# Recurrent attention and a gated MLP on one core: scores and the state's product in one stretch, placed between the two groups of y

## The chip, the cores and the metric

The kernel runs on one core of a Trainium2 chip. The core has five engines that work side by side: TensorE (PE, matrix products into PSUM), VectorE (DVE), ScalarE (ACT), GpSimd (POOL) and SyncE (SP, which issues the DMAs). Each runs its own list of instructions in order, and waits on semaphores where it needs another engine's result. The metric is the device time of one execution in microseconds, the median of several runs.

## The reference

For 4 sequences, 8 heads, 768 positions and head size 48, a state of 48x48 per head is carried along the positions; the result is the input of a gated MLP with mixing over positions (gMLP, d_model 384, d_ff 1024):

```
for t in range(S):
    cur = einsum('bhd,bhe->bhde', u * k_t, v_t)
    y[t] = einsum('bhd,bhde->bhe', r_t, state + cur)
    state = w_t[..., None] * state + einsum('bhd,bhe->bhde', k_t, v_t)
x = y, heads side by side                      # (4, 768, 384)
h = gelu(x @ w_in);  u, v = halves of h
v_n = (v - mean) / sqrt(var + 1e-6) * g_ln
v_s = einsum('ts,bsd->btd', w_sg, v_n) + b_sg
out = x + (u * v_s) @ w_out
```

## The kernel before

**Steps.** The recurrence is cut into chunks of 128 positions: 6 per sequence, 24 steps in all, counted from 0 (step n is chunk n % 6 of sequence n // 6). A chunk has two halves of 64 positions. The 8 heads lie as 4 pairs, one head of a pair in partitions 0 to 63, the other in 64 to 127. Per step:

- loads of w, of k and r (KR), of v, and from step 6 on of k and r once more in another layout (RK, for the "own weights");
- `decays`, `decayed_k`: two scans over the decays on DVE (lines 430 and 435), then k and r multiplied by their decays (lines 459 and 437, DVE or POOL);
- `own_weights`: the term u*k*r of each position with itself. For the first ON_PE["own"] steps one product on DVE or POOL and 4 matmuls (line 473), after that three elementwise operations on RK. The result fills the diagonal of the tile `a`;
- `scores`: 16 matmuls of 64x64 (k against r, line 506) into the PSUM buffer a_ps; then DVE copies what lies under the mask into `a` (line 508);
- `state`: 4 transposes of k (line 520) into k_ps, a copy to SBUF (kt), 16 matmuls of 64x48 (kt against v, line 529) into a_ps, and three operations of DVE or POOL: S1 = product of the first half + S2 (line 540), T2 = S1 times a decay (line 546), S1' = product of the second half + T2 (line 552). `decayed` makes the next step's S2 from S1' (line 565 or 563). On the chip each matmul of this data type gives two records in the trace, so 16 matmuls are 32 records;
- `outputs`: y in one PSUM buffer, in two groups. The first group is 8 matmuls of `a` and v (line 581); the second is 8 or 16 matmuls of the states S2 and T2 with r (line 602) and 8 more of `a` and v (line 581). Between the groups a copy of one column of y, the "look" (line 593, on ACT or DVE; a copy helper, so the trace shows it as line 283) is awaited by PE, so that the second group starts only when the first can be read. Three copies then take y to SBUF.

a_ps is a single buffer of two banks, taken twice per step: once by the scores, once by the state's product. kt is a single buffer too.

**gMLP.** Each product in full precision is made of three passes (lines 681 to 683) over matmuls of 128x128 weights and 384 or 512 columns, in three PSUM buffers (m_ps). `v_piece`: the v half of one chunk, GELU and normalisation; `u_piece`, `gate_piece` (18 passes over all six v of a sequence), `out_piece` with its final sum on DVE (line 779, into one of two buffers o) and the DMA out (line 781). The weights come in as 64-bit numbers and are split into a high and a low part; for the first ON_PE["w"] of ten weights the low part is gathered by three passes on PE (lines 816 to 818) and a copy, for others by two elementwise operations on POOL or DVE (lines 823 and 825).

**What sets the order.** All this is written as generators that yield operations (`Op`) with a cost per engine, events they wait for, and buffers they take. `Plan.run` keeps a clock per engine and always picks the operation that can start first; among those that can start within 0.02 us of each other the lower rank wins. A step's rank is n - LEAD of its sequence; gMLP pieces have ranks from the constants FIRST and PIECE, weights from WEIGHT. The order so found is fixed at build time; on the chip each engine follows it. `small` marks stretches of 64x64 matmuls: in the plan the first such operation after a full matmul costs 0.1 us more. `_, done, e_...` are events; an operation sees another's result `LAT` after its end (0.3 us after PE, 0.2 after others).

Of the kernel before, what the change touches and what calls it, by code (L numbers as in the profile page):

```python
# [14 lines left out]
ALU = mybir.AluOpType  # L15
# [4 lines left out]
B, H, S, D = 4, 8, 768, 48  # L20
C = 128
T = 64
NC = S // C
NP = H // 2
# [11 lines left out]
LEAD = (2.97, 1.57, 3.33, 2.58)  # L36
FIRST = {"v": -1.8, "u": 4.09, "gate": 1.92, "out": 6.86}
PIECE = {"v": 1.71, "u": 3.76, "gate": 4.87, "out": 1.55}
WEIGHT = {"v": -10.85, "u": -4.28, "sg0": 2.68, "sg1": -0.01, "out": -0.36, "g": 4.14}

BIAS = {"DVE": 0.07, "POOL": -0.09}
# [33 lines left out]
class Op:  # L75
# [3 lines left out]
    def __init__(self, on, after=(), take=(), free=(), done=None, kb=None, two=False, apart=False, small=False, slack=0.0):  # L79
        self.on, self.after, self.take, self.free, self.done, self.kb = on, after, take, free, done, kb  # L80
        self.two = two
        self.slack = slack
        self.small = small
        self.apart = apart
# [6 lines left out]
class Event:  # L91
    t = None

# [35 lines left out]
class Plan:  # L129
# [13 lines left out]
    def cost(self, op, e, t):  # L143

        c = op.on[e]
        if e == "PE":
            c = (2 * c if t < COLD else c) + (0.1 if op.small and not (self.pe_last and self.pe_last.small) else 0.0)
        return c

    def add(self, rank, gen):  # L150
        self.count += 1
        p = [rank, gen, 0.0, None, self.count]
        self.procs.append(p)
        self._next(p, None)
# [7 lines left out]
    def run(self):  # L162
        while True:
            best = {}
            for p in self.procs:
                op = p[3]
                if any(e.t is None for e in op.after) or any(len(s.free) < op.take.count(s) for s in op.take):
                    continue
                ready = max([p[2]] + [e.t for e in op.after] + [s.since(op.take.count(s)) for s in op.take])
                _, t, e = min((s + self.cost(op, e, s) + BIAS.get(e, 0.0), s, e) for e in op.on  # L170
                              for s in (max(ready, self.engines[e], self.port if op.port(e) else 0.0),))
                best.setdefault(e, []).append((t, p[0], p[4], p))
# [24 lines left out]
            if op.done is not None:  # L197
                op.done.t = op.seen
            if not op.apart:
                p[2] = op.seen  # L200
# [75 lines left out]
def rwkv_gmlp(ctx: ExitStack, tc: tile.TileContext, wpad, kr, vtok, ktok, vt, u, ucol, w_in, g_ln, w_sgT, b_sg, w_out, out):  # L276
# [5 lines left out]
    def copy(e, o, i):  # L282
        nc.scalar.copy(o, i) if e == "ACT" else engine[e].tensor_copy(o, i)  # L283
# [103 lines left out]
    ch = [Part("W", "KR", "V", "RK", "own", "k", "r", "suf", "pre", "pc", "A", "M", "S1", "S2", "T2", "ym", "y") for _ in steps]  # L387
# [74 lines left out]
    def own_weights(n):  # L462

        x = ch[n]
        if n < ON_PE["own"]:
# [4 lines left out]
            op = yield Op({"PE": 0.8}, small=True, after=[e_uc], take=[m_m], free=[rk])  # L470
# [27 lines left out]
    def scores(n):  # L498

        x = ch[n]  # L500
        op = yield Op({"PE": 0.62}, small=True, after=[x.e_k, x.e_r], take=[m_a])
        a_ps, = op.got
        x.kr.done(op.seen)
        for p, j, c_ in [(p, j, c_) for p in range(NP) for j in range(2) for c_ in range(2)]:
            k_, r_ = (x.KR[64 * j:64 * j + 64, i, p * C + c_ * T:p * C + c_ * T + T] for i in range(2))
            nc.tensor.matmul(a_ps.tile[64 * c_:64 * c_ + 64, j, p * T:(p + 1) * T], k_, r_, start=True, stop=True)  # L506
        yield Op({"DVE": 0.64}, after=[x.e_A], free=[a_ps], done=x.e_M)
        nc.vector.copy_predicated(x.a.tile.rearrange("s j p t -> s j (p t)"), mask, a_ps.tile[:, :, 0:NP * T])

    def state(n):  # L510
# [4 lines left out]
        m = T if last else C  # L515
        op = yield Op({"PE": 0.37}, after=[x.e_k], take=[m_s])
        kt_ps, = op.got
        x.kr.done(op.seen)
        for p in range(NP):
            nc.tensor.transpose(kt_ps.tile[0:m, p], x.KR[:, 0, p * C:p * C + m], ident)  # L520
        op = yield Op({"ACT": 0.5, "DVE": 0.61}, take=[s_kt], free=[kt_ps])
        kt, = op.got
        copy(op.e, kt.tile[0:m], kt_ps.tile[0:m])
        op = yield Op({"PE": 0.4 if last else 0.62}, small=True, after=[x.e_V], take=[m_a], free=[kt])
        ds, = op.got
        x.v.done(op.seen)
        for p, c_, j in [(p, c_, j) for p in range(NP) for c_ in range(1 if last else 2) for j in range(2)]:
            h = 2 * p + j
            nc.tensor.matmul(ds.tile[64 * j:64 * j + 64, c_, p * 64:p * 64 + D],  # L529
                             kt.tile[64 * c_:64 * c_ + 64, p, 64 * j:64 * j + 64],  # L530
                             x.V[64 * c_:64 * c_ + 64, h * D:(h + 1) * D], start=True, stop=True)
        ds_ps = [ds.tile[:, c_, 0:NP * 64].rearrange("d (p e) -> d p e", e=64)[:, :, 0:D] for c_ in range(2)]
        ds.n = 1 if last else 2
        mid = ds_ps[0]
        if g > 0:
            op = yield Op({"DVE": 0.27}, after=[x.e_S2], take=[s_S1], free=[ds])
            S1, = op.got
            mid = S1.tile
            x.S2.done(op.seen)
            nc.vector.tensor_tensor(mid, ds_ps[0], x.S2.tile[:, :, 0:D], ALU.add)  # L540
        op = yield Op({"DVE": 0.3, "POOL": 0.6} if g else {"DVE": 0.3}, after=[x.e_pc], take=[s_S2], done=x.e_T2,
                      free=[S1 if g else ds], two=g > 0)
# [3 lines left out]
        engine[op.e].tensor_tensor(x.T2.tile[:, :, 0:D], mid,  # L546
                                   x.pc.tile[:, :, 1].unsqueeze(2).broadcast_to([128, NP, D]), ALU.mult)
        if not last:
            op = yield Op({"DVE": 0.27}, take=[s_S1], free=[ds], done=x.e_S1)
            x.S1, = op.got  # L550
            x.T2.done(op.seen)
            nc.vector.tensor_tensor(x.S1.tile, ds_ps[1], x.T2.tile[:, :, 0:D], ALU.add)
# [16 lines left out]

    def outputs(n):  # L570
# [15 lines left out]
        op = yield Op({"PE": 0.36}, small=True, after=[x.e_M, x.e_V, *turn], take=[m_y])  # L586
# [179 lines left out]
    def out_piece(b, half, i):  # L766
# [10 lines left out]
        op = yield Op({"DVE": 0.48}, take=[s_o], free=[m, h_.x])  # L777
# [117 lines left out]
    for n, (b, g) in enumerate(steps):  # L895
# [6 lines left out]
        for f in (decays, range_check, chunk_pc, decayed_k, own_weights, state, decayed, scores, outputs):  # L902
            if f is decayed and g == 0:
                continue
            plan.add(r, f(n))
# [210 lines left out]
```

## Time and profile before

| | |
|---|---|
| time, median of 3 runs | 391.02 us (389.45 to 391.55) |
| time of the profiled execution | 392.47 us |
| its span, first to last instruction | 390.6 us |
| granted TensorE clock, mean | 0.994 |
| PE busy | 363.0 us (93%), 4513 matmul records |
| weight loads (PEld) busy | 317.2 us (81%) |
| DVE, ACT, POOL busy | 292.1 (75%), 193.2 (49%), 93.7 us (24%) |
| HBM read and written | 43.19 and 4.72 MB |

The span counts from the first to the last instruction of the program; the time of an execution holds a little more around it. Busy is the share of time in which at least one instruction of the engine is drawn. Matmuls are pipelined, so two of them overlap in the drawing; the distance from start to start tells more than the duration.

### The profile page before, as it was taken

To read this page: it belongs to the slowest core of one execution; us is meant where nothing else is said; L and a number is where in the kernel's file an instruction comes from. 1 tells how busy PE (TensorE), PEld (TensorE's weight loads), DVE (VectorE), ACT (ScalarE), POOL (GpSimd) and SP (SyncE) were. 2 spreads that over 40 slices of the span, in tenths; PEclk is the share of its full clock that TensorE was granted. 3 is DMA by queue.
4 is the path that set the end of the run, shared out by engine and by line. 5 is a ranking of instruction groups with operands and counts; after the bars stand their busy time and mean duration, and the time that the engine had idled before them with its cause. 6 is when DMAs were issued, how large, how long until landed. Compare 5 with 4: busy or idle time off the path is not lost.

```text
span 390.6 us, 10968 instructions
## 1 busy us (share of the span) xinstructions
PE 363.0 (93%) x4513; PEld 317.2 (81%) x4513; DVE 292.1 (75%) x588; ACT 193.2 (49%) x502; POOL 93.7 (24%) x121
## 2 busy tenths in 40 slices
PE   1989899799989999999999999999999999989992
PEld 1756678588879978978799988878999889979991
DVE  7999998699999979998999797487732545452251
ACT  3659676785432565666344166563444744521010
POOL 6124441233142254225540332032000002100000
PEclk9999999999999999999999999999999999999997
DMA  8776558624356254663323713122325510000101
GB/s 264 275 235 195 165 152 287 205 88 143 86 171 213 64 160 147 225 220 100 120 90 128 229 48 121 45 76 90 112 94 184 160 56 25 3 1 20 42 1 67
DMA packets 23961, 49.87 MB, mean 128 GB/s; under 512 B 3808, under 2 KB 12768, under 8 KB 23904
## 3 DMA queue, kind: packets, MB, share of 16 engines
q1 hardware_dynamic: 23904, 49.10, 38.4%
q8 instruction: 37, 0.61, 0.6%
q14 instruction: 20, 0.16, 0.1%
HBM read 43.19 MB, written 4.72 MB: 123 GB/s over the span
## 4 chain that ended last, share of the span: by engine, by line
PE 70%; DVE 17%; DMA 6%; ACT 3%; issue 2%; ACTq 0%; DVEq 0%
PE m_ps L681 20%; PE m_ps L683 17%; PE m_ps L682 17%; PE a_ps L506 3%; PE y_ps L581 3%; PE a_ps L529 2%; PE y_ps L602 2%; DVE m_ps L757 2%; PE k_ps L520 2%; DMA u<-in_w_sgT 2%; DVE W L435 2%; DVE a L495 2%; DVE W L430 1%; DMA x<-y 1%; DMA KR<-in_kr 1%
## 5 line engine op out<-in xcount | busy, mean ns | idle before, releaser
L681 PE MATMUL m_ps<-wsgh,vn 128*128 128x384 f32 x192 | 67.9, 353 | 2.6 <-DVE g L763 2.6
L683 PE MATMUL m_ps<-wsgh,vn 128*128 128x384 f32 x192 | 64.7, 337 | 0.1
L682 PE MATMUL m_ps<-wsgl,vn 128*128 128x384 f32 x192 | 64.6, 336 | 0.0
L681 PEld LDWEIGHTS m_ps<-wsgh,vn 128*128 128x128 f32 x192 | 36.0, 188 | 5.6 <-DVE g L763 3.6
L761 ACT CAST g<-m_ps 128x384 fp32r<-128x384 f32 x32 | 15.2, 480 | 44.9 <-DVE m_ps L759 44.6
L683 PEld LDWEIGHTS m_ps<-wsgh,vn 128*128 128x128 f32 x192 | 36.1, 188 | 0.4 <-DVE vn L723 0.4
L682 PEld LDWEIGHTS m_ps<-wsgl,vn 128*128 128x128 f32 x192 | 36.1, 188 | 0.3
L712 POOL TENSOR_TENSOR st<-st,mhalf 128x1 f32<-128x1 f32 x24 | 20.4, 853 | 62.3 <-DVE st L710 50.6
L757 DVE SCALAR_TENSOR_TENSOR m_ps<-m_ps,g_ln,b_bc 128x384 f32<-128x384 f32 x32 | 19.3, 619 | 20.0 <-PE m_ps L683 20.0
L681 PE MATMUL m_ps<-g,wouth 128*128 128x384 f32 x96 | 34.0, 354 | 0.0
L681 PE MATMUL m_ps<-xT,winh 128*128 128x384 f32 x96 | 33.5, 348 | 0.1
L446 ACT ACTIVATE junk<-W 128x1040 f32<-128x1040 f32 x24 | 25.8, 1073 | 14.9 <-DVE W L435 12.2
L682 PE MATMUL m_ps<-g,wouth 128*128 128x384 f32 x96 | 32.5, 338 | 0.5 <-DVE g L763 0.5
L683 PE MATMUL m_ps<-xT,winl 128*128 128x384 f32 x96 | 32.4, 337 | 0.0
L683 PE MATMUL m_ps<-g,woutl 128*128 128x384 f32 x96 | 32.3, 337 | 0.0
L682 PE MATMUL m_ps<-xT,winh 128*128 128x384 f32 x96 | 32.3, 337 | 0.0
L430 DVE TENSOR_TENSOR_SCAN W<-W,D 128x520 f32<-128x520 f32 x24 | 30.8, 1283 | 1.7 <-DMA W<-in_wpad 1.7
L737 ACT ACTIVATE u<-m_ps 128x384 f32<-128x384 f32 x32 | 15.6, 490 | 31.8 <-PE m_ps L683 31.7
L435 DVE TENSOR_TENSOR_SCAN W<-W,D 128x520 f32<-128x520 f32 x24 | 31.1, 1297 | 0.1
L681 PE MATMUL m_ps<-winh,xT 128*128 128x512 f32 x72 | 31.1, 432 | 0.2 <-DVE g L763 0.2
L683 PE MATMUL m_ps<-winh,xT 128*128 128x512 f32 x72 | 28.6, 397 | 0.8 <-ACT xT L283 0.8
L682 PE MATMUL m_ps<-winl,xT 128*128 128x512 f32 x72 | 28.4, 394 | 0.0
(151 smaller groups left out, 837.6 us busy)
## 6 DMA issues: line engine op xcount, KB each, us to landing
KR<-in_kr SPq DMA_DIRECT2D x24, 512.0 KB, 4.2
RK<-in_ktok SPq DMA_DIRECT2D x18, 384.0 KB, 3.7
W<-in_wpad SPq DMA_DIRECT2D x24, 260.5 KB, 3.6
vtok<-in_vtok SPq DMA_DIRECT2D x24, 192.0 KB, 4.2
out<-o SPq DMA_DIRECT2D x24, 192.0 KB, 1.9
vn<-in_w_in SPq DMA_DIRECT2D x6, 512.0 KB, 6.1
KR<-in_w_in SPq DMA_DIRECT2D x6, 512.0 KB, 3.8
u<-in_w_sgT SPq DMA_DIRECT2D x12, 192.0 KB, 3.9
```

The source lines that it names most:

```text
L430: nc.vector.tensor_tensor_scan(Suf[:, WL - 1:0:-1], W[:, WL - 1:0:-1], D1[:, WL - 1:0:-1], 0.0, ALU.mult, ALU.add)
L435: nc.vector.tensor_tensor_scan(W[:, 0:WL - 1], W[:, 0:WL - 1], D2[:, 0:WL - 1], 0.0, ALU.mult, ALU.add)
L446: nc.scalar.activation(junk.rearrange("p (a x) -> p a x", a=2), both, AF.Square, accum_out=chk[:, n:n + 1])
L506: nc.tensor.matmul(a_ps.tile[64 * c_:64 * c_ + 64, j, p * T:(p + 1) * T], k_, r_, start=True, stop=True)
L581: nc.tensor.matmul(place(j, q, r, c_), x.V[64 * c_:64 * c_ + 64, h * D:h * D + 64], x.a.tile[64 * c_:64 * c_ + 64, j, p], start=(start and ...
L681: nc.tensor.matmul(ps, lh, rh, start=(i == 0), stop=False)
L682: nc.tensor.matmul(ps, lh, rl, start=False, stop=False)
L683: nc.tensor.matmul(ps, ll, rh, start=False, stop=(i == n - 1))
L712: nc.gpsimd.tensor_tensor(rstd, var, c.mhalf, ALU.pow)
L737: nc.scalar.activation(h_.u[f].tile, ps, AF.Gelu_apprx_tanh)
L757: nc.vector.scalar_tensor_tensor(ps, ps, c.g[:, d:d + 1], c.b_bc[:, ts], ALU.mult, ALU.add)
L761: nc.scalar.copy(gh, ps)
```

## The change

The scores and the state's product of a step become one operation, `products`: 32 matmuls back to back into one a_ps buffer (scores in the first half of each bank, the state's product in the second). The transposes and the copy kt become an operation of their own (`turned_k`), the masked copy another (`masked`). For steps 0 to 9 (JOINED = 9) `first_products` runs the products by themselves. For the later ones they are part of `outputs` of the step before: from step 9 on the order on PE is first group of y of step n, products of step n+1, second group of y of step n, each marked `next_to` (rank lowered by 100). For this the first group also waits for all that the second group and the products need. The look is a process of its own, with its rank lowered by 50.

In the planner, an operation that follows one on its own engine may start at that one's end, without the latency; entering a small stretch costs 0.2; constants are new. One more step has its own weights on PE, two weights fewer have their low part there. The last half's outputs use buffers of u in place of o.

```diff
-ON_PE = {"own": 6, "x": 5, "w": 10}
+JOINED = 9
+ON_PE = {"own": 7, "x": 5, "w": 8}
...
-            c = (2 * c if t < COLD else c) + (0.1 if op.small and not (self.pe_last and self.pe_last.small) else 0.0)
+            c = (2 * c if t < COLD else c) + (0.2 if op.small and not (self.pe_last and self.pe_last.small) else 0.0)
...
-                ready = max([p[2]] + [e.t for e in op.after] + [s.since(op.take.count(s)) for s in op.take])
+                ready = max([0.0] + [s.since(op.take.count(s)) for s in op.take])
                 _, t, e = min((s + self.cost(op, e, s) + BIAS.get(e, 0.0), s, e) for e in op.on
-                              for s in (max(ready, self.engines[e], self.port if op.port(e) else 0.0),))
-                best.setdefault(e, []).append((t, p[0], p[4], p))
+                              for s in (max([ready, self.engines[e], self.port if op.port(e) else 0.0, p[2].on(e)]
+                                            + [x.on(e) for x in op.after]),))
+                best.setdefault(e, []).append((t, p[0] - (100.0 if op.next_to else 0.0), p[4], p))
...
+    def products(n, op):
+        x = ch[n]
+        last = steps[n][1] == NC - 1
+        x.ps, = op.got
+        ps, kt = x.ps.tile, x.kt.tile
+        for p, j, c_ in [(p, j, c_) for p in range(NP) for j in range(2) for c_ in range(2)]:
+            k_, r_ = (x.KR[64 * j:64 * j + 64, i, p * C + c_ * T:p * C + c_ * T + T] for i in range(2))
+            nc.tensor.matmul(ps[64 * c_:64 * c_ + 64, j, p * T:(p + 1) * T], k_, r_, start=True, stop=True)
         for p, c_, j in [(p, c_, j) for p in range(NP) for c_ in range(1 if last else 2) for j in range(2)]:
             h = 2 * p + j
+            nc.tensor.matmul(ps[64 * j:64 * j + 64, c_, NP * T + p * T:NP * T + p * T + D],
+                             kt[64 * c_:64 * c_ + 64, p, 64 * j:64 * j + 64],
                              x.V[64 * c_:64 * c_ + 64, h * D:(h + 1) * D], start=True, stop=True)
+        for buf in (x.kr, x.v, x.kt):
+            buf.done(op.seen)
+        x.ps.n = 2 if last else 3
+
+    ready = lambda n: [ch[n].e_k, ch[n].e_r, ch[n].e_V, ch[n].e_kt]
...
+        with_it = ready(n + 1) if n + 1 < N else []
...
-        op = yield Op({"PE": 0.36}, small=True, after=[x.e_M, x.e_V, *turn], take=[m_y])
+        joined = n >= JOINED
+        final = [x.e_T2, x.e_r, *([x.e_S2] if g else [])]
+        op = yield Op({"PE": 0.27}, small=True, after=[x.e_M, x.e_V, *turn, *([*final, *with_it] if joined else [])],
+                      take=[m_y])
...
-        op = yield Op({"ACT": 0.2, "DVE": 0.1}, take=[s_look])
-        look, = op.got
-        copy(op.e, look.tile, y.tile[0][:, 1, C - 1:C])
-        look.done(op.seen)
-        op = yield Op({"PE": 0.87 if g else 0.63}, small=True, after=[x.e_T2, x.e_r, *([x.e_S2] if g else [])],
-                      done=x.e_ym)
+        e_look = Event()
+        plan.add(rank(n) - 50.0, look(y, e_look, op.seen))
+        if joined and with_it:
+            op = yield Op(time(n + 1), small=True, take=[m_a], done=ch[n + 1].e_sd, next_to=True)
+            products(n + 1, op)
+        op = yield Op({"PE": 0.79 if g else 0.55}, small=True, after=[e_look, *final], done=x.e_ym, next_to=joined)
...
-        op = yield Op({"DVE": 0.48}, take=[s_o], free=[m, h_.x])
+        op = yield Op({"DVE": 0.48}, take=[s_u if h_.n == N - 3 else s_o], free=[m, h_.x])
```

## Rows read from the trace of the kernel before

**Rows 1.** Busy time by engine in three windows: stretch, length, busy (x instructions), clock, DMA.

```profile
0.00:62.00 62.00, 48.84 (x834) 36.40 (x835) 58.17 (x108) 39.91 (x111) 23.20 (x39) 1.00 0.67 220
62.00:200.00 138.00, 133.11 (x1912) 115.14 (x1911) 126.69 (x248) 77.15 (x203) 45.22 (x50) 1.00 0.47 152
200.00:320.00 120.00, 119.83 (x1439) 107.57 (x1438) 80.48 (x171) 58.28 (x148) 21.28 (x26) 1.00 0.34 112
```

**Rows 2.** Waits of PE: who waited for whom, us in total, times, longest.

```profile
PE m_ps L681 <- DVE g L763: 2.8, 4, 1.6
...
PE y_ps L581 <- DVE a L508: 1.2, 2, 0.9
```

**Rows 3.** Timeline of PE about a first group of y: start, us drawn, instruction.

```profile
182.85 0.34 PE L682 MATMUL m_ps<-wsgl,vn 128*128 128x384 f32 x1
183.02 0.34 PE L683 MATMUL m_ps<-wsgh,vn 128*128 128x384 f32 x1
183.29 0.46 PE L581 MATMUL y_ps<-a,vtok 64*64 64x64 f32 x16
...
183.96 0.34 PE L682 MATMUL m_ps<-wsgl,vn 128*128 128x384 f32 x1
```

**Rows 4.** Timeline of PE about a second group of y that stands alone.

```profile
212.86 0.34 PE L683 MATMUL m_ps<-wsgh,vn 128*128 128x384 f32 x1
213.12 0.69 PE L602 MATMUL y_ps<-KR,S 64*64 64x64 f32 x32
213.64 0.41 PE L581 MATMUL y_ps<-a,vtok 64*64 64x64 f32 x16
...
214.26 0.34 PE L682 MATMUL m_ps<-wsgl,vn 128*128 128x384 f32 x1
```

**Rows 5.** Timeline of PE where a state's product stands between the groups of y.

```profile
167.59 0.46 PE L581 MATMUL y_ps<-a,vtok 64*64 64x64 f32 x16
167.87 0.63 PE L529 MATMUL a_ps<-vtok,kt 64*64 64x48 f32 x32
168.42 0.69 PE L602 MATMUL y_ps<-KR,S 64*64 64x64 f32 x32
168.91 0.44 PE L581 MATMUL y_ps<-a,vtok 64*64 64x64 f32 x16
```

**Rows 6.** Timeline of PE: the second group of y of steps 5 and 23.

```profile
63.74 0.69 PE L602 MATMUL y_ps<-KR,S 64*64 64x64 f32 x32
...
316.46 0.69 PE L602 MATMUL y_ps<-KR,S 64*64 64x64 f32 x32
```

**Rows 7.** Timeline of PE: own weights of a step, and one weight of w_out.

```profile
46.46 0.95 PE L473 MATMUL m_ps<-u_col,RK 128*128 128x8 f32 x8
...
70.92 0.91 PE L816 MATMUL m_ps<-g,ident 128*128 128x384 f32 x2 [1.71 <-ACT u L737]
...
72.02 0.34 PE L681 MATMUL m_ps<-xT,winh 128*128 128x384 f32 x1
```

**Rows 8.** Two lines' instructions: count, ns min/median/max, first and last start.

```profile
L676 DVE TENSOR_TENSOR xT<-x,xT x19: 508/551/1067, 77.9 to 329.7; 128x384 fp32r<-128x384 f32 x19
...
L481 POOL TENSOR_TENSOR RK<-RK,u_bc x11: 997/1027/1471, 74.4 to 204.5; 128x384 f32<-128x384 f32 x11
```

**Rows 9.** Timeline of PE, DVE and ACT: a first group of y, two looks.

```profile
171.31 0.46 PE L581 MATMUL y_ps<-a,vtok 64*64 64x64 f32 x16
...
172.60 0.14 DVE L283 COPY look<-y_ps 128x1 f32<-128x1 f32 x1
...
183.82 0.16 ACT L283 COPY look<-y_ps 128x1 f32<-128x1 f32 x1 [1.05 <-PE y_ps L581]
```

**Rows 10.** Timeline of all engines at the end.

```profile
382.70 0.34 PE L683 MATMUL m_ps<-g,woutl 128*128 128x384 f32 x1
383.76 0.56 DVE L779 TENSOR_TENSOR o<-m_ps,x 128x384 f32<-128x384 f32 x1 [2.24 <-DMA out<-o]
```

**Rows 11.** Timeline of DVE: the last normalised v.

```profile
342.86 0.69 DVE L723 TENSOR_TENSOR vn<-v,vn 128x512 fp32r<-128x512 f32 x1 [0.69 <-ACT vn L283]
```

More of the change, by code (lines that the diff above doesn't have):

```diff
@@ L75, with __init__ @@
 class Op:
-    def __init__(self, on, after=(), take=(), free=(), done=None, kb=None, two=False, apart=False, small=False, slack=0.0):
+    def __init__(self, on, after=(), take=(), free=(), done=None, kb=None, two=False, apart=False, small=False, slack=0.0,
+                 next_to=False):
         self.on, self.after, self.take, self.free, self.done, self.kb = on, after, take, free, done, kb
         self.two = two
+        self.next_to = next_to
         self.slack = slack
@@ L196, in run @@
                 b.done(op.seen)
[L197 to L200, printed above, removed]
+            for x in [p[2]] * (not op.apart) + [op.done] * (op.done is not None):
+                x.t = op.seen
+                if op.kb is None:
+                    x.e, x.end = e, op.end
             self.log.append((t, op.end, e, p[0], p[1].__name__))
@@ L496, in own_weights, with turned_k @@
                                        diag.unsqueeze(1).unsqueeze(1).broadcast_to([128, 2, NP, T]), ALU.mult)
-    def scores(n):
+    def turned_k(n):
         x = ch[n]
-        op = yield Op({"PE": 0.62}, small=True, after=[x.e_k, x.e_r], take=[m_a])
-        a_ps, = op.got
+        m = T if steps[n][1] == NC - 1 else C
+        op = yield Op({"PE": 0.37}, after=[x.e_k, *([ch[n - 1].e_kt] if n else [])], take=[m_s])
+        kt_ps, = op.got
         x.kr.done(op.seen)
+        for p in range(NP):
+            nc.tensor.transpose(kt_ps.tile[0:m, p], x.KR[:, 0, p * C:p * C + m], ident)
+        op = yield Op({"ACT": 0.5, "DVE": 0.61}, take=[s_kt], free=[kt_ps], done=x.e_kt)
+        x.kt, = op.got
+        copy(op.e, x.kt.tile[0:m], kt_ps.tile[0:m])
@@ new lines, in products, with first_products, masked @@
+        for buf in (x.kr, x.v, x.kt):
+            buf.done(op.seen)
+        x.ps.n = 2 if last else 3
+    ready = lambda n: [ch[n].e_k, ch[n].e_r, ch[n].e_V, ch[n].e_kt]
+    time = lambda n: {"PE": 0.78 if steps[n][1] == NC - 1 else 1.02}
+    def first_products(n):
+        op = yield Op(time(n), small=True, after=ready(n), take=[m_a], done=ch[n].e_sd)
+        products(n, op)
+    def masked(n):
+        x = ch[n]
+        op = yield Op({"DVE": 0.64}, after=[x.e_A, x.e_sd], done=x.e_M)
+        x.ps.done(op.seen)
+        nc.vector.copy_predicated(x.a.tile.rearrange("s j p t -> s j (p t)"), mask, x.ps.tile[:, :, 0:NP * T])
@@ L568, in decayed, with look @@
         x.pc.done(op.seen)
+    def look(y, done, t):
+        e = Event()
+        e.t = t
+        op = yield Op({"ACT": 0.2, "DVE": 0.1}, take=[s_look], after=[e], done=done)
+        look, = op.got
+        copy(op.e, look.tile, y.tile[0][:, 1, C - 1:C])
+        look.done(op.seen)
     def outputs(n):
@@ L901, in rwkv_gmlp @@
             plan.add(FIRST_LOADS.get((n, f.__name__), r), f(n))
-        for f in (decays, range_check, chunk_pc, decayed_k, own_weights, state, decayed, scores, outputs):
-            if f is decayed and g == 0:
+        for f in (decays, range_check, chunk_pc, decayed_k, turned_k, own_weights, first_products, masked, state, decayed,
+                  outputs):
+            if f is decayed and g == 0 or f is first_products and n > JOINED:
                 continue
```

66 lines of the change are left out of this document (27 added, 39 removed).

## The prediction

> **What bounds the kernel now.** I read the windows of three stretches first. TensorE (PE) is busy 133.11 of 138 us between 62 and 200 us and 119.83 of 120 us between 200 and 320 us, at the full granted clock, while VectorE (DVE) falls from 126.69 of 138 to 80.48 of 120 [rows 1]. Before 62 us PE has gaps (48.84 of 62), since inputs and decays are still arriving. The list of waits agrees: of PE's later waits the largest is 2.8 us in all, for the gate's product g, and for the step's own operands y waited 1.2 us [rows 2]. So from about 62 us on PE always has a gMLP product ready, and time taken out of PE's queue there comes off the end. A busy share can't say how much is useful, though: a 384-column product is drawn 0.34 us long but the next one starts 0.17 us later [rows 3]. I therefore go by starts.
>
> The timeline of PE shows what small products cost beside their own work. Small ones (64 rows by 64 columns) stand in stretches between full ones (128 by 128). Within a stretch they start 0.016 us apart (32 in 213.12 to 213.64, [rows 4]). The first group of y, alone, takes from 183.02 to 183.96, the starts of the full product before it and of the second one after it: 0.94 us. Two full ones take 2 x 0.17, the 16 small ones 16 x 0.016 = 0.26, and 0.34 is left over [rows 3]. The second group, 48 small ones alone: 1.40 - 0.34 - 0.77 = 0.29 [rows 4]. Both ends are one price: entering and leaving a stretch costs about 0.31 us, however long it is.
>
> One place already looks as the changed kernel will: at 167.59 the state's product stands directly between the two groups of y, and 16 + 32 + 32 products go from 167.59 to 168.91, 1.32 us or 0.04 over 80 x 0.016 [rows 5]. Two seams, 0.02 each. Joining two stretches therefore saves 0.31 - 0.02 = 0.29 us.
>
> **The change part by part.** *Stretches.* Steps are counted from 0. From the second group of y of step 5 at 63.74 to the last at 316.46 I count 61 stretches of small products between full ones [rows 6]. Up to four per step: scores, state's product, first and second group of y; some touch by chance. In the changed kernel the same part holds: the second y of step 5, two groups each for steps 6 to 8, one stretch of products each for steps 6 to 9 (11 in all); one stretch each for steps 9 to 22 with the products of the next step inside (14); two groups of step 23. That is 27. Chance merges among the 11 may take 2 away, and some of the 14 will be split because a condition isn't met in the plan (4 more). I take 29, with 25 and 45 as ends. 61 - 29 = 32 stretches x 0.29 = 9.3 us less. The number of small products, of transposes and of DVE's instructions per step is the same, and so are their times.
>
> *Before 62 us* there were 16 stretches, where PE waits anyway. Scores now also wait for the turned k and for v, and the state's product for r. I cost this at nothing, hidden by those 13.2 us of gaps, with 2 us either way; a gain or a loss there ends in the same idle time.
>
> *Fewer weights on PE* (10 to 8). Two of w_out lose three passes: 70.92 to 72.02 is 1.10 us each [rows 7], 2.2 us less on PE. In their place come two elementwise operations each (lines 823 and 825), which no row of before shows. The nearest are a 128x384 subtraction on DVE, 0.55 us, and a 128x384 product on GpSimd, 1.03 us [rows 8], so 2.2 us of DVE or 4.1 of GpSimd, less one copy each. Neither is on the path: nothing asks for w_out before the first output product, and PE has other work. Bounds 0 and +2.2, I take 0.
>
> Beside GpSimd's work that DVE row goes up to 1.07 us from a median of 0.55 [rows 8]. The Trainium skill (SBUF — State Buffer, Who interferes with whom) says why: a DVE instruction with two inputs in SBUF is kept out while a GpSimd instruction that reads SBUF runs, for its whole length. The trace agrees in kind; by that rule alone DVE would lose up to the 4.1 us, and 4.1 us more on the end if DVE set it.
>
> *Own weights of step 6 on PE* (6 to 7): eight more products, 0.95 us [rows 7], against a DMA of 384 KB and two elementwise operations less. +0.95.
>
> *The look* (the one-column copy that PE awaits between the groups of y) had other full products as cover; now it has the 64 products, 64 x 0.016 = 1.0 us. An early one starts 0.53 us after its group's start and is done at 183.98, 0.69 after it [rows 3, 9], and the first group itself lasts 0.26, so 0.43 is needed of 1.0. The late one ran on DVE at 172.60, behind a copy, its group having begun at 171.31; it is done at 172.74, 1.43 after [rows 9]: that would leave PE idle 1.43 - 0.26 - 1.0, about 0.2 us plus the way back. Of the 15 looks from step 9 on this was the only late one. I allow 14 x 0.02 = 0.3.
>
> *The joint gate.* The first group of y of step n now waits for what the second needed (the state before and in the middle of the chunk) and for k, r, v and the turned k of step n+1, and the buffer must be free of its three readers. PE works in order, so every full product behind a gate that is late waits, and after it the copies out of the three m_ps buffers. The rows give 0.9 us as the longest such wait for y [rows 2]. Steps are 14 us apart (18 between 63.74 and 316.46, [rows 6]) and only three or four DVE operations lie between products and gate, so the gate is normally met long ahead. I allow 0.7 us in all; bounds 0 and 14 x 0.45 (half of the longest) = 6.3.
>
> *The order* is made anew with other constants, and an operation after one on its own engine no longer counts a latency. What can be won so is PE's idle time from 62 to 320 us, 4.9 + 0.2 = 5.1 us [rows 1]; what can be lost I put into the rivals. I take 0.
>
> *The end.* The last sum of the output waits for a buffer that a DMA holds: DVE starts at 383.76, the last product ended at 382.70 + 0.34 = 383.04 [rows 10]. With the last half's outputs in the eight u buffers it starts at once: 0.7 us less. What follows (DMA out, closing waits) stays.
>
> Sum: -9.3 - 2.2 + 0.95 + 0.3 + 0.7 - 0.7 = -10.25. The profiled execution took 392.47 us (span 390.6 and 1.9 around it), so 382.2; it was 1.45 above the median of the runs, 391.02. From the median: 380.8 us.
>
> **The rivals.**
> *D, stretches not whole.* The planner takes whatever can start first; when the buffer or the look is a moment late, full products slip in and a joint stretch falls into two or three. The many chance splittings of before speak for it, and that the new operations get precedence once ready speaks against. With half of the gain: 16 x 0.29 = 4.6, so 385.4.
> *B, waits at the gate.* All the stretches come whole, but 14 gates or looks cost 0.45 us rather than 0.07: 5.3 back, 386.1. For it: a static order with ten conditions at one point; against: a single long wait for y in the trace.
> *E, no change.* D and B together: 4.7 + 5.3 back, 390.8.
> *C, slower: DVE takes over the path between 62 and 200 us.* It has 11.3 us free there [rows 1]; a PE that is some 6 us ahead brings gMLP's sums and casts forward into the same stretch, the two w_out weights add theirs, and the step's mask and state sums then come in one burst after the products, on which the next gate hangs. Then the attention falls behind, and the last y is late. After it comes a chain that can't be moved: the last normalised v is ready at 342.86 + 0.69 = 343.55 [rows 11], and 39.5 us of gate and output products follow up to 383.04. From the last y (ends about 317.3) to 343.55 are 26 us; I put half of them, 13 us, down as slack (an estimate). So the kernel becomes slower than before only if the last y comes after about 333 us. At 336 the span is 336 + 13 + 39.5 + 6.9 = 395.4, and the time 395.4 + 1.9 - 1.45 = 396. Against it: DVE has 39.5 us free from 200 to 320 to catch up. The rule of the Trainium skill cited above belongs here; by its 4.1 us alone that point would not be reached.
>
> **How the numbers follow.** Forecast 0.60, D 0.13, B 0.13, E 0.06, C 0.08. I call 0.5% (2 us) no change, what a measurement here can tell. Faster by more: 0.60 + 0.13 + 0.13 = 0.86; within: 0.06; slower: 0.08. The forecast's own range is 377 to 384 (28 or 36 stretches saved, 2 us at the start, a part of the 5.1 us of idle time). The range of 8 in 10 takes in D and B and reaches towards E: 375.5 to 389.
>
> **What would show it.** In the timeline of PE: 27 to 33 stretches of small products after the second y of step 5, and from step 9 on the row order y, scores, state, y with no full product between; starts within it 0.016 us apart. PE's busy time down by some 9 to 11 us, its products' number down by two weights' passes and up by eight. No idle row before L581 or the second group beyond 0.5 us. The last y near 306 us; the last output sum right behind its product. Wrong would be: over 40 stretches (D), idle rows summing over 4 us at y (B), DVE without gaps and the last y after 325 us (C), or a stretch price that doesn't go away when stretches are joined.

## The result and the profile after

The changed kernel takes 385.86 us (median of 4 runs, 385.12 to 387.65), the kernel before 391.05 (4 runs): ratio 0.9881, 95% interval 0.9836 to 0.9926. It is faster by 5.2 us, half of the 10.25 us forecast. The profiled execution took 385.56 us with a span of 383.9.

The page of the changed kernel, busy time by engine, and its windows (columns as in [rows 1]):

```profile
PE 353.7 (92%) x4513; PEld 317.6 (83%) x4513; DVE 307.0 (80%) x593; ACT 191.5 (50%) x507; POOL 106.4 (28%) x144
```

```profile
0.00:62.00 62.00, 45.72 (x672) 32.86 (x675) 56.57 (x99) 27.41 (x67) 19.21 (x36) 0.92 0.59 198
62.00:200.00 138.00, 132.61 (x2069) 119.56 (x2062) 134.37 (x257) 86.35 (x249) 53.57 (x60) 1.00 0.49 154
200.00:320.00 120.00, 118.02 (x1470) 109.69 (x1469) 88.05 (x180) 63.07 (x160) 28.52 (x37) 1.00 0.35 117
```

PE is busy 9.3 us less, as forecast, but DVE 14.9 us more, with hardly more to do (593 instructions against 588). The 14.9 has two parts. The drawn times of DVE's instructions add up to 328.5 us before and 336.4 after, 7.9 more; and of this sum 36.4 us overlap before and 29.5 after, 6.9 less. The first part is instructions drawn longer while GpSimd works: 29 before and 39 after took over 0.06 us more than the median of their kind in all runs, 15.4 and 22.9 us more in sum, and every one of them had a GpSimd instruction beside it. Against [rows 1] PE did less in the first 62 us (672 matmul records instead of 834, at a clock of 0.92 instead of 1.00), and DVE has lost nearly all of its free time between 62 and 200 us: 138 - 134.37 = 3.6 us instead of 11.3.

The stretches came nearly as planned: of the 14 joint ones 12 are whole, and two (steps 12 and 20) are split by three or four products of 128 rows. Timeline of PE about a joint one of the changed kernel (L618 is y of `a` and v, L531 the scores, L534 the state's product, L642 y of states and r):

```profile
173.13 0.40 PE L723 MATMUL m_ps<-winh,xT 128*128 128x512 f32 x1
173.46 0.46 PE L618 MATMUL y_ps<-a,vtok 64*64 64x64 f32 x16
173.74 0.65 PE L531 MATMUL a_ps<-KR 64*64 64x64 f32 x32
174.21 0.63 PE L534 MATMUL a_ps<-vtok,kt 64*64 64x48 f32 x32
174.66 0.66 PE L642 MATMUL y_ps<-KR,S 64*64 64x64 f32 x32
175.14 0.41 PE L618 MATMUL y_ps<-a,vtok 64*64 64x64 f32 x16
175.48 0.50 PE L721 MATMUL m_ps<-winh,xT 128*128 128x512 f32 x1
```

From 173.46 to 175.48 there are 128 records and 2.02 us, 0.0158 each with the seams inside, against 0.016 within the short stretches of [rows 3, 4]. By the count of the prediction, from the second group of y of step 5 on, 27 stretches are left instead of 61.

The list of waits of PE in the changed kernel (who waited for whom, us in total, times, longest) answers [rows 2]:

```profile
PE m_ps L484 <- DVE RK L480: 8.3, 2, 7.5
PE m_ps L856 <- DVE vn L845: 4.6, 3, 3.0
PE y_ps L642 <- DVE look L294: 2.5, 3, 1.4
PE k_ps L517 <- DVE KR L470: 2.4, 4, 1.3
PE y_ps L618 <- DVE a L552: 1.8, 3, 1.3
```

The 7.5 is the start, as long before the change. These five, the longest of the list, all wait for DVE: for the own weights' product, the low parts of the first weights, the look, the decayed k, the mask.

Where the 6.7 us of span went (from the start of each matmul to that of the next, less the median distance for its shape, summed over each trace): entering and leaving stretches 27.3 before, 15.1 after, -12.2; all other excess 21.7 before, 26.8 after, +5.1, of which the first 62 us are +6.7 and the rest -1.7; the matmuls themselves and the rest +1.5; from PE's end to the span's end 7.56 before, 6.5 after, -1.1. (With every wait of PE over 0.15 us put to the other excess, the stretches give 28.5 and 17.5, so -11.0.) So the gain from the stretches is larger than forecast, and about half of it is lost again at the start.

**What DVE does there.** Timeline of DVE in the changed kernel (L843 to L851 split one piece of w_in into high and low part, four operations each on the result of the one before; L552 is the masked copy of step 0):

```profile
13.16 0.40 DVE L843 TENSOR_SCALAR vn<-vn 128x512 int32<-128x512 int32 x1
13.60 0.69 DVE L845 SCALAR_TENSOR_TENSOR vn<-vn,vn 128x512 int32<-128x512 int32 x1
14.32 0.43 DVE L849 TENSOR_SCALAR vn<-vn 128x512 int32<-128x512 int32 x1
...
18.62 0.42 DVE L843 TENSOR_SCALAR vn<-vn 128x512 int32<-128x512 int32 x1
19.08 0.69 DVE L845 SCALAR_TENSOR_TENSOR vn<-vn,vn 128x512 int32<-128x512 int32 x1
19.80 0.43 DVE L849 TENSOR_SCALAR vn<-vn 128x512 int32<-128x512 int32 x1
20.27 0.69 DVE L851 SCALAR_TENSOR_TENSOR winl<-vn,vn 128x512 fp32r<-128x512 uint32 x1
20.88 0.72 DVE L552 COPY_PREDICATED a<-mask,a_ps 128x512 f32<-128x512 uint8 x1
```

The state's product of step 0, the end of the stretch whose scores the mask copies, had run long before:

```profile
11.88 1.05 PE L534 MATMUL a_ps<-vtok,kt 64*64 64x48 f32 x32
```

The same stretch of DVE in the kernel before (L508 is the mask, L803 to L811 the same four operations):

```profile
12.51 0.73 DVE L508 COPY_PREDICATED a<-mask,a_ps 128x512 f32<-128x512 uint8 x1
...
14.11 0.41 DVE L803 TENSOR_SCALAR vn<-vn 128x512 int32<-128x512 int32 x1
14.44 0.41 DVE L809 TENSOR_SCALAR vn<-vn 128x512 int32<-128x512 int32 x1
14.78 0.68 DVE L805 SCALAR_TENSOR_TENSOR vn<-vn,vn 128x512 int32<-128x512 int32 x1
```

Two things differ. The chains of the weights run through in one piece, one after another, and the mask of step 0 comes behind all three, at 20.88 instead of 12.51 us, though its scores were there by 12.93 us: it is DVE's order that holds it back, not the products. And in a chain each instruction starts only after its predecessor's drawn end (13.16 + 0.40 = 13.56, next 13.60), while independent neighbours overlap (14.11 + 0.41 = 14.52, next 14.44): about 0.12 us of DVE per pair. Before 200 us I count 13 neighbours spaced like a chain in the kernel before and 98 in the changed one: 85 x 0.12 = 10 us.

PE then waits, and its clock drops. Timeline of PE, of GpSimd and DVE ahead of PE's longest wait, and two windows of the changed kernel:

```profile
19.82 1.12 PE L856 MATMUL m_ps<-vn,ident 128*128 128x512 f32 x2
...
29.49 2.07 PE L856 MATMUL m_ps<-vn,ident 128*128 128x512 f32 x2 [2.99 <-DVE vn L845]
```

```profile
27.55 1.33 POOL L480 TENSOR_TENSOR RK<-KR 128x512 f32<-128x512 f32 x1 [11.64 <-DMA KR<-in_kr]
27.76 1.67 DVE L845 SCALAR_TENSOR_TENSOR vn<-vn,vn 128x512 int32<-128x512 int32 x1
```

```profile
26.00:29.00 3.00, 0.50 (x32) 0.37 (x28) 2.93 (x5) 1.16 (x2) 1.33 (x1) 1.00 0.48 175
29.00:32.00 3.00, 2.51 (x4) 1.38 (x5) 2.86 (x6) 0.90 (x2) 0.00 (x0) 0.57 0.03 6
```

About 1 us of the 2.99 is not the chain: beside GpSimd the L845 that PE waits for is drawn 1.67 us, where it takes 0.69 alone (13.60 above).

**What could make chains.** The planner's new rule, `Event.on`: an operation behind one on its own engine may start at that one's end, with no latency. For the planner the next instruction of a chain on DVE can then start at once, earlier than anything that waits for another engine, and it picks what can start first.

### The profile page after: what moved, and what is told of

Same layout as the page of the kernel before. It is cut to its first block, busy times and chain, and to the rows that moved or that the text cites. A ratio compares the mean times of both kernels' runs of the same rounds, so it can differ in the third digit from the quotient of the medians.

```text
span 383.9 us, 11011 instructions
## 1 busy us (share of the span) xinstructions
PE 353.7 (92%) x4513; PEld 317.6 (83%) x4513; DVE 307.0 (80%) x593; ACT 191.5 (50%) x507; POOL 106.4 (28%) x144
## 4 chain that ended last, share of the span: by engine, by line
PE 50%; DVE 37%; DMA 5%; issue 4%; SPq 1%; ACT 1%; DVEq 0%; ACTq 0%
PE m_ps L721 15%; PE m_ps L723 14%; PE m_ps L722 14%; DVE W L441 4%; DVE W L446 4%; DVE a L552 2%; DMA x<-y 2%; DVE KR L448 2%; DVE KR L470 2%; PE y_ps L618 2%; DVE xT L716 2%; PE y_ps L642 2%; DVE S L572 1%; PE k_ps L517 1%; DMA vtok<-in_vtok 1%
## 5 line engine op out<-in xcount | busy, mean ns | idle before, releaser
L721 PE MATMUL m_ps<-wsgh,vn 128*128 128x384 f32 x192 | 65.3, 340 | 0.0
L723 PE MATMUL m_ps<-wsgh,vn 128*128 128x384 f32 x192 | 64.6, 336 | 0.0
L801 ACT CAST g<-m_ps 128x384 fp32r<-128x384 f32 x32 | 15.3, 479 | 55.9 <-DVE m_ps L799 55.9
L457 ACT ACTIVATE junk<-W 128x1040 f32<-128x1040 f32 x24 | 25.7, 1072 | 19.3 <-DVE W L446 10.8
L446 DVE TENSOR_TENSOR_SCAN W<-W,D 128x520 f32<-128x520 f32 x24 | 32.7, 1363 | 0.5
L721 PE MATMUL m_ps<-g,wouth 128*128 128x384 f32 x96 | 33.1, 345 | 0.0
L722 PE MATMUL m_ps<-g,wouth 128*128 128x384 f32 x96 | 32.4, 338 | 0.6 <-DVE g L803 0.6
L752 POOL TENSOR_TENSOR st<-st,mhalf 128x1 f32<-128x1 f32 x24 | 15.9, 662 | 59.6 <-DVE st L750 54.3
L441 DVE TENSOR_TENSOR_SCAN W<-W,D 128x520 f32<-128x520 f32 x24 | 30.6, 1276 | 1.6 <-DMA W<-in_wpad 1.6
L492 POOL TENSOR_TENSOR RK<-RK,u_bc 128x384 f32<-128x384 f32 x17 | 22.7, 1337 | 5.2 <-DMA RK<-in_ktok 5.0
```

What stands on the lines that cost most here:

```text
L441: nc.vector.tensor_tensor_scan(Suf[:, WL - 1:0:-1], W[:, WL - 1:0:-1], D1[:, WL - 1:0:-1], 0.0, ALU.mult, ALU.add)
L446: nc.vector.tensor_tensor_scan(W[:, 0:WL - 1], W[:, 0:WL - 1], D2[:, 0:WL - 1], 0.0, ALU.mult, ALU.add)
L457: nc.scalar.activation(junk.rearrange("p (a x) -> p a x", a=2), both, AF.Square, accum_out=chk[:, n:n + 1])
L492: engine[op.e].tensor_tensor(t[:, 0], t[:, 0], u_bc, ALU.mult)
L721: nc.tensor.matmul(ps, lh, rh, start=(i == 0), stop=False)
L722: nc.tensor.matmul(ps, lh, rl, start=False, stop=False)
```

## The experiments

Theory A: the rule `Event.on` does the damage through DVE. Theory B: the joined products do, since the scores now wait for the turned k. Theory C: neither; any new order differs by so much. Below, "chain neighbours" are DVE's neighbours spaced like a chain before 200 us (the next start 0 to 0.12 us after the drawn end), "stretches" those from the second group of y of step 5 on, its own included (61 before, 27 after). Ratios are to the kernel before, with their 95% interval.

**1. The changed kernel without the rule.**

```diff
-        return self.end if e == self.e else self.t
+        return self.t
```

> The changed kernel with one thing undone in the planner: an operation sees the end of one on its own engine with the latency again (0.2 us on DVE), so the order is made anew. Theory A (the new rule lets DVE run chains of dependent instructions one behind the other: such an instruction starts about 0.04 us after the end of the one before, an independent one 0.08 us before it, and the attention's work waits behind whole chains of weight splitting, so that PE starves in the first 62 us): dependent neighbours on DVE before 200 us fall from 98 to under 35, PE busy in 0 to 62 us rises from 45.7 to 48 us or more, the second y of step 5 comes before 68 us (74.66 now), the time is 380 to 383 us. Theory B (the start is slower because scores now wait for the turned k and for v): all of this stays, 385 to 387.5 us.

402.34 us, ratio 1.0287 (1.0228 to 1.0347). Chain neighbours 98 to 20, and the second y of step 5 comes at 65.7 us instead of 74.7 (63.7 before): so far A. But A's time, 380 to 383 us, is missed by 19 us: the stretches rise to 53, and between 62 and 200 us PE is idle 14.3 us. The rule is also what keeps products and y together on PE (run 10 shows it). This kernel loses the rule and keeps constants that were made for it, so its time alone decides nothing.

**2. The kernel before, with the rule only.** The edit is the class `Event` and `run` of the change, nothing else.

> The kernel before with only the new rule for dependencies on one engine in its planner. Theory A: dependent neighbours on DVE before 200 us rise from 13 to over 70, the start slows (second y of step 5 after 68 us, 63.74 before), 394 to 398 us. Theory B: no such effect, 389 to 392.5 us.

406.67 us, ratio 1.0391 (1.0325 to 1.0458), chain neighbours 101, the second y of step 5 at 82.3 us, PE idle 17.0 us before 62 us. The rule alone makes the chains and slows the start. The size, 9 us past what A expected, again holds the constants in it.

**3. The kernel before, with the buffers of the last outputs only.**

```diff
-        op = yield Op({"DVE": 0.48}, take=[s_o], free=[m, h_.x])
+        op = yield Op({"DVE": 0.48}, take=[s_u if h_.n == N - 3 else s_o], free=[m, h_.x])
```

> The kernel before with only the last half's outputs in u's buffers. Both theories: only the end moves, the last sum right behind its product, 0.7 us less (0.4 to 1.2): about 390.3 us.

390.11 us (10 runs), ratio 0.9971 (0.9943 to 0.9998): 1.1 us by the ratio, as the tail of the changed kernel shows. The changed kernel's last rows, answering [rows 10]:

```profile
377.05 0.33 PE L723 MATMUL m_ps<-g,woutl 128*128 128x384 f32 x1
377.42 0.56 DVE L819 TENSOR_TENSOR u<-m_ps,x 128x384 f32<-128x384 f32 x1 [1.52 <-PE m_ps L723]
```

**4. The changed kernel with scores and state's product apart in steps 0 to 9.**

```diff
-        for f in (..., own_weights, first_products, masked, ...):
+        for f in (..., own_weights, scores_first, state_first, masked, ...):
```

`scores_first` waits for k and r only, `state_first` for v and the turned k; the mask waits for the scores.

> The changed kernel with scores and state's product as two stretches for steps 0 to 9, the rest as changed. Theory B: the start is as fast as before (second y of step 5 near 64 us), 381 to 383 us in spite of up to ten stretches more. Theory A: the start stays slow, and the added stretches cost up to 10 x 0.29 us where PE is the bound: 385.5 to 389 us.

393.49 us, ratio 1.0055 (1.0026 to 1.0084). The start is as slow as ever (second y of step 5 at 83.6 us, PE idle 19.1 us before 62). Taking the extra wait of the scores away doesn't bring the start back, so B falls. A's range for the time, 385.5 to 389, is missed too, by 4.5 us; why the start is slower still than in the changed kernel isn't shown (the scores and the state's product take the single a_ps in turn here).

**Constants made for each kernel.** For the runs that follow the constants (LEAD, FIRST, PIECE, WEIGHT, BIAS, ON_PE) were searched for each kernel so that its own plan becomes short; the search knows the planner's costs and nothing of the chip. ON_PE also moves some work between the engines, so two such kernels differ by a little work of PE as well: up to 4 us among runs 5 to 12, estimated from the median distances of starts; between runs 6 and 8 it is 0.6, and run 11, one of the fastest, has the most.

**5. The rule on PE alone**, elsewhere the latency as before.

```diff
-        return self.end if e == self.e else self.t
+        return self.end if e == self.e == "PE" else self.t
```

> The changed kernel with the rule (no latency after an operation on one's own engine) for PE alone, and LEAD, FIRST, PIECE, WEIGHT, BIAS and ON_PE chosen anew so that the plan is short under that rule. The stretches of y, products, y need the rule on PE; DVE gets its latency of 0.2 us back. Theory A (the rule on DVE hides 0.12 us per dependent pair and lets chains run in front of the attention, and that ate half of the gain): joint stretches stay (under 32 after the second y of step 5), dependent neighbours on DVE before 200 us under 35, idle rows of PE before 62 us at most 14 us, and the time comes to 374 to 380 us. Theory C (every new order differs by chance by some per cent, and the changed kernel's is simply what it got): anything from 384 to 400 us.

376.28 us, ratio 0.9584 (0.9546 to 0.9622); stretches 26, chain neighbours 22, PE idle 13.0 us before 62 us.

**6. The rule with a price**: nothing on PE, 0.12 us on any other engine, what the spacing of DVE shows.

```diff
-        return self.end if e == self.e else self.t
+        return self.end + (0.0 if e == "PE" else 0.12) if e == self.e else self.t
```

> As the one with the rule on PE alone, but an operation behind one that it needs on the same engine is counted 0.12 us later on DVE, ACT and POOL (what the trace shows on DVE), with its own constants. Theory A: 373 to 380 us, dependent neighbours on DVE before 200 us between 20 and 70. Theory C: 384 to 400 us.

372.79 us, ratio 0.9529 (0.9497 to 0.9561): the fastest version, 13 us under the changed kernel. Stretches 29, chain neighbours 14, fewer than the 20 to 70 expected. Its page and first window, beside those of the changed kernel above:

```profile
PE 347.1 (94%) x4503; PEld 313.9 (85%) x4503; DVE 292.1 (79%) x605; ACT 192.8 (52%) x499; POOL 93.3 (25%) x119
```

```profile
0.00:62.00 62.00, 48.32 (x819) 36.29 (x819) 58.51 (x118) 37.77 (x92) 17.51 (x35) 1.00 0.70 225
62.00:200.00 138.00, 134.19 (x1954) 121.95 (x1954) 130.05 (x262) 79.56 (x212) 55.50 (x55) 1.00 0.49 152
```

DVE is back at the 292.1 us of the kernel before with 17 instructions more, PE has 819 records in the first 62 us again, and its clock stays at 1.00.

**7. The changed kernel, its full rule, constants anew.**

> The changed kernel with its rule as it is, and only the constants chosen anew in the same way. Theory A: the constants don't cure it, dependent neighbours on DVE before 200 us stay above 80, PE's idle rows before 62 us above 14 us, 383 to 390 us. Theory C: the same spread as for the others, no better and no worse than the two with another rule.

386.92 us, ratio 0.9891 (0.9853 to 0.9929); chain neighbours 98. Constants don't cure it. The first window:

```profile
0.00:62.00 62.00, 46.15 (x736) 31.20 (x736) 55.04 (x92) 33.13 (x95) 20.79 (x39) 1.00 0.59 193
```

PE is idle 15.8 us there, nearly as in the changed kernel, but at the full clock.

**8. The kernel before, constants anew.**

> The kernel before with only the constants chosen anew in the same way: what a new order alone gives, with no joint stretches. Theory A: some 60 stretches after the second y of step 5, so not under 384; 384 to 390 us. If it came under 382 us, the order and not the stretches would be the larger part.

384.18 us, ratio 0.9804 (0.9780 to 0.9827); stretches 61, chain neighbours 19. Two windows:

```profile
0.00:62.00 62.00, 46.70 (x771) 35.45 (x772) 56.49 (x109) 39.39 (x107) 23.45 (x40) 0.92 0.73 242
62.00:200.00 138.00, 137.36 (x1928) 120.39 (x1927) 129.42 (x249) 80.97 (x223) 62.19 (x61) 1.00 0.48 149
```

New constants alone are worth 7 us on the kernel before. So the comparison for the joined products is run 6 against this one, 11.4 us, and not either against the original.

**9. The kernel before with the full rule, constants anew for it.** The edit of run 2.

> The kernel before, with nothing of the change but the planner's rule that an operation sees its own engine's results at once, and its constants chosen anew for that rule in the same manner as in e8_before_constants. Theory A (the rule makes DVE run chains of dependent instructions, and that costs the start): slower than e8 (384.2) although the plan it was chosen for is shorter: 388 to 400 us, dependent neighbours on DVE before 200 us above 70. Rival (the rule is harmless once the constants fit it, and e2 was slow only because they did not): 380 to 385, near e8. If that rival holds, e7 against e6 must be put down to something else.

394.92 us, ratio 1.0080 (1.0053 to 1.0106); chain neighbours 97. With nothing of the joined products in it, the rule costs 10.7 us against run 8. Its page shows the same sign, DVE's busy time with 585 instructions; the second line is its window from 62 to 200 us:

```profile
PE 361.1 (92%) x4494; PEld 315.1 (80%) x4494; DVE 306.7 (78%) x585; ACT 195.7 (50%) x513; POOL 101.8 (26%) x135
```

```profile
62.00:200.00 138.00, 129.84 (x1797) 113.55 (x1795) 129.04 (x251) 74.14 (x195) 46.83 (x52) 1.00 0.47 148
```

Where the loss lies differs from the changed kernel: PE is idle 16.2 us before 62 us against run 8's 15.3, but 8.2 us between 62 and 200 against 0.6.

**10. The changed kernel without the rule, constants anew for that.** The edit of run 1.

> The changed kernel without the rule on any engine, constants chosen anew for it. Theory A's other half (on PE the rule is needed, since without it the products and the second group of y wait out a latency in the plan and full products slip in): stretches after the second y of step 5 at 40 to 55 instead of 28, DVE's dependent neighbours before 200 us under 30, start as in the kernel before (second y of step 5 near 64), and (28 against some 48 stretches) x 0.29 = 6 us more than e6_rule_priced: 377 to 383. Rival (the joint operation as such loses, whatever the rule): 388 or more.

385.16 us, ratio 0.9843 (0.9763 to 0.9922), 2 us past the expected end; chain neighbours 15, stretches 54. Not one joint stretch is whole. Timeline of PE at step 11, where the changed kernel had one stretch:

```profile
141.40 0.46 PE L618 MATMUL y_ps<-a,vtok 64*64 64x64 f32 x16
141.79 0.50 PE L721 MATMUL m_ps<-winh,xT 128*128 128x512 f32 x1
...
142.68 0.69 PE L531 MATMUL a_ps<-KR 64*64 64x64 f32 x32
143.19 0.63 PE L534 MATMUL a_ps<-vtok,kt 64*64 64x48 f32 x32
143.75 0.50 PE L721 MATMUL m_ps<-winh,xT 128*128 128x512 f32 x1
...
144.65 0.34 PE L642 MATMUL y_ps<-KR,S 64*64 64x64 f32 x8
```

With a latency of 0.3 us counted after the first group in the plan, a full product can start earlier than the products, so it is put between, whatever their rank. Joined like this the change wins nothing over run 8.

**11. Run 6 with a second choice of constants.**

> e6_rule_priced with its constants chosen a second time from another start of the search, nothing else: how much two choices for one and the same kernel differ. If the comparisons among kernels with their own constants mean something: 370 to 377, and DVE's dependent neighbours before 200 us under 30. If such choices scatter by 8 us or more, e5 to e8 tell less than I take from them.

373.67 us, ratio 0.9533 (0.9478 to 0.9588); stretches 27, chain neighbours 24. Two choices for one kernel differ by 0.9 us, and the differences of 10 us among runs 5 to 12 are far above that, so C has little left. Only for this kernel was the choice repeated.

**12. Run 6 with the products as one stretch in every step, but never put between the groups of y.**

```diff
-JOINED = 9
+JOINED = 99
```

> e6_rule_priced with scores and state's product of a step as one stretch for every step, but nowhere put between the two groups of y of the step ahead; constants chosen for it. By the price of 0.29 us per stretch: up to 23 + 48 stretches less chance merges, some 55 to 60 after the second y of step 5 against 28, so (57 - 28) x 0.29 = 8.4 us slower than e6_rule_priced: 378 to 384, close to e8 (384.2). Rival (joining scores and state's product is most of the gain, the place between the groups adds little, since the gate's ten conditions cost what the seams save): 372 to 376.

382.74 us, ratio 0.9784 (0.9723 to 0.9845); stretches 49, fewer than the 55 to 60 expected. Placing the products between the groups of y gains 10 us (20 stretches fewer, 0.5 us each). Against run 8 this kernel, with the products joined and the priced rule, gains 1.4 us for 12 stretches fewer, 0.12 each. So the price of a stretch doesn't give the time of either step by itself; only their sum, 11.4 us for 32, 0.36 each, agrees with it.

| own constants each | no rule | full rule | rule on PE, 0.12 us elsewhere |
|---|---|---|---|
| kernel before | 384.18 | 394.92 | not run |
| changed, products apart from y | not run | not run | 382.74 |
| changed | 385.16 | 386.92 | 372.79, 373.67 |

Read by rows: the full rule costs the kernel before 10.7 us against no rule. It costs the changed one 1.8 against no rule, which is within the spread of run 10's times, and 13 to 14 against the priced one, since there the rule on PE is needed and the rule on DVE harms. Read by columns: without the rule the change wins nothing, with the full rule 8.0, and with the priced one placing the products between the groups wins 10. The kernel before was not run with the priced rule, so of the 11.4 us between runs 8 and 6 the part that the priced rule alone would give is not known.

## Why the prediction was half right

**Stretches: right, and a little small.** 27 came where 29 were forecast. The account of starts gives 12.2 us (11.0 without waits) for 34 stretches fewer over the whole trace, 0.36 (0.32) each, where 0.29 was taken. Runs 6 and 8 repeat it: 26.1 to 14.7 us for 74 to 43 in all, 0.37 each.

**Weights: right.** After 62 us the passes of the weights take 2.4 us less by starts (2.2 forecast). **The end: right**, 1.1 us for 0.7; the last sum starts 0.04 after the last product's drawn end.

**Gate and look.** From step 9 on, where both stand, PE waited over 0.15 us at y only once: for a look on DVE, 1.45 us, where 1.0 was allowed for both kinds. The other long rows at y, 1.27 us at 97.13 (the mask) and 0.67 at 126.28 (a look), belong to steps 6 and 8, whose products stand by themselves. The late look in the changed kernel:

```profile
138.64 0.46 PE L618 MATMUL y_ps<-a,vtok 64*64 64x64 f32 x16
...
141.28 0.14 DVE L294 COPY look<-y_ps 128x1 f32<-128x1 f32 x1
141.47 0.34 PE L642 MATMUL y_ps<-KR,S 64*64 64x64 f32 x7 [1.45 <-DVE look L294]
```

The group began at 138.64, the look ran 2.64 us later, when DVE came free. This is the late look of [rows 9] again, on a fuller DVE. By the mark that I had set for B (over 4 us at y) the waits at y, 2.5 + 1.8 in the list, are just past it, but only 1.45 us of them stand in a joint stretch, so B is not what cost the time.

**The step that failed** is the pair of terms put at nothing: "Before 62 us ... I cost this at nothing, hidden by those 13.2 us of gaps", with 2 us either way, and under the order, "no longer counts a latency ... I take 0". The gaps of PE before 62 us are no cover, because most of them are DVE's. In the kernel before, 10.8 us of PE's waits there ended with DVE, above all these two, and [rows 1] has DVE busy 58.17 of those 62 us:

```profile
PE m_ps L473 <- DVE RK L469: 7.5, 1, 7.5
PE a_ps L506 <- DVE S L552: 1.8, 1, 1.8
```

What makes DVE later there makes PE later. In the changed kernel the first 62 us cost 6.7 us more than before. PE's idle time there rose from 13.2 to 16.3 us, and runs 1 and 2 tie this to the rule: 13.2 us in the changed kernel without it, 17.0 in the kernel before with it. The rest goes along with PE's clock, 0.92 over the 62 us, which is at most 5 us of full speed (an estimate, 0.08 x 62). It fell after the longest wait, so that two matmul records that took 1.12 us at 19.82 took 2.07 at 29.49, and twice more:

```profile
47.00:50.00 3.00, 3.00 (x93) 2.73 (x86) 1.80 (x5) 1.17 (x3) 1.77 (x4) 0.52 0.61 163
56.00:59.00 3.00, 3.00 (x12) 2.36 (x12) 2.93 (x7) 2.71 (x8) 1.22 (x1) 0.62 0.71 241
```

That the rule brings the low clock is not shown: run 7 has the rule and 1.00 over the first 62 us, run 8 has no rule and 0.92. I read the new rule as a matter of the plan's arithmetic, and did not ask on which engine it would change who goes first.

**DVE beside GpSimd.** The prediction named up to 4.1 us of DVE for the two weights' share of this and added none. DVE's instructions were held up by 7.5 us more than before (22.9 against 15.4). This alone does not set the time: run 11 has 22.2 us of it and takes 373.67 us.

**Rival C** named the right engine and the wrong way. DVE did lose its free time between 62 and 200 us, with 9 instructions more there (257 against 248), so more through chains and slower instructions than through sums and casts brought forward, and it did not hold up the attention to the end: the last y came earlier than forecast, 299.81 us against 306 (316.46 in [rows 6]):

```profile
299.81 0.69 PE L642 MATMUL y_ps<-KR,S 64*64 64x64 f32 x32
```

**Rival D** needs the rule's absence: in run 10 the stretches fall apart as D had it, in the changed kernel they don't; that both land near D's 385.4 is chance.

**What stays open.** That the full rule costs 10.7 us and more is shown; by which way, only in part. It does two things at once: it lets chains go first, so that the mask comes late, and it makes DVE pay 0.12 us per pair. Runs 5 and 6 undo both. No run keeps the chains and takes away their price, or the reverse; 85 x 0.12 = 10 us of DVE is of the size of the loss (10.7 in run 9), which does not prove it. Run 9 also has more of DVE's time lost beside GpSimd than run 8, 23.2 against 16.3 us, and its loss lies mostly behind 62 us, unlike that of the changed kernel. Why run 8 is 7 us shorter than the kernel before, at as many stretches, I didn't look into beyond PE's idle rows (4.9 us between 62 and 200 before, 0.6 there).

## What to carry to other kernels

Where a gap of one engine is to hide a cost, see first which engine makes the gap: what delays that one is not hidden. In an order made by a greedy planner a latency is also a right of way; setting it to zero hands the engine to whatever chain is running, so change it engine by engine, with the spacing that the trace shows for that engine. And judge such an edit with constants made for each side: here runs 1 and 2, with constants made for another rule, were 17 and 12 us slower than the same kernels with their own (runs 10 and 9), more than the effect looked for.

## What the runs showed of the hardware

DVE's spacing falls into two groups. From a drawn end to the next start, in steps of 0.02 us, the kernel before has 396 of some 590 neighbours at -0.08 us and 29 at +0.04; the changed one 307 and 129. Of those between 0.02 and 0.06 us, 29 of 33 before and 127 of 132 after had waited for a semaphore of the instruction right before them. The Trainium skill (VectorE: DVE Perf Modes, The DRAIN you can't avoid) has the next operation wait until the pipe is empty, says that one which is not held starts earlier, and gives eight copies the same time with a semaphore after each as with one after the last. The rows here agree that some start earlier, and put a number to it: an instruction that does not wait for the one before it starts 0.12 us sooner. No run here repeats the eight copies.

DVE was slowed only beside GpSimd. In all 14 traces together, every DVE instruction that was drawn over 0.06 us longer than the median of its kind (39 in the changed kernel, 29 in the kernel before) had an instruction of GpSimd beside it; in the rows above one took 1.67 us (27.76) instead of 0.69.

The granted clock of PE was 1.00 in the windows of the first 62 us of the kernel before. In the changed one it was 0.57 from 29 to 32 us, right behind a wait of 2.99 us (PE was busy 0.50 of the 3 us from 26 to 29): most of that window at 1.2 GHz, the rest at 2.4. From 35 to 38 us it was 1.00 again. It fell twice more, 0.52 from 47 to 50 and 0.62 from 56 to 59 us, with no wait over 0.9 us in the 10 us before either.
